# Ninety-nine small loads that nothing reads, beside a stream of large ones

## The chip, the cores and the metric

The kernel runs on one core of one Trainium2 chip. The metric is the device time of one execution in microseconds (us), the median of several. The core has TensorE (PE in the profile), VectorE (DVE), ScalarE (ACT), GpSimd (POOL) and SyncE (SP), and 16 DMA engines that move data between the device memory and the core's own memory. SP, ACT and POOL can issue loads; each has a queue of its own.

## The reference

A decode step for two sequences, one token each: attention over a cache of 4096 positions, beside a feed-forward layer, mixed by a gate.

```python
q = (x @ wq)                                  # 2 x 1 x 448 -> 16 heads of 256
scores = einsum("bhqd,bhkd->bhqk", q, k_cache) * 256 ** -0.5
p = softmax(scores)
a = einsum("bhqk,bhkd->bhqd", p, v_cache) @ wo
h = relu(x @ w1 + b1) ** 2
b = h @ w2 + b2
g = sigmoid((x * gate_w).sum(-1))
out = g * a + (1 - g) * b                     # 2 x 1 x 448
```

All is float32. The K cache and the V cache have 2 x 16 x 4096 x 256 numbers each, 134 MB each; the weights are small beside them.

## The kernel before, in words

The work goes in 16 rounds. A round is two heads of one sequence: its K is 8.4 MB and its V is 8.4 MB, each laid over 128 partitions, 64 positions of 256 numbers in each. Three buffers of that size fill most of the core's memory: `kp[0]` and `kp[1]` for the K of even and odd rounds, `vp` for V. At the start and at the end the same buffers hold wq, w1, wo and w2.

In a round i, VectorE multiplies K with the query in place (`times_q`, line 403), and sums each row of 256 products (`row_sums`, line 408), in two halves: multiply, sum, multiply, sum. The sums are the scores; they go to `s_t[i % 2]`, called `s0` and `s1`, so `s1` holds the scores of the odd rounds. Then come the maximum over all partitions (lines 420 and 430, with a turn through TensorE), the exponentials on ScalarE (`softmax`, line 437), and on TensorE 64 matrix products with V (`values`). Every fourth round the result is normalized and multiplied with a part of wo.

The main loop (`for i in range(LOOPED)`, lines 575 to 600) covers i = 0 to 11; the last four rounds are written out below it. In each pass it issues on SP: V of round i, K of round i + 2, and in every fourth pass a part of wo. Then come the products with V of round i, and VectorE's work on round i + 1.

SP issues in the order of the text and waits before each load until its buffer is free. V of round i goes into `vp`, free once TensorE has done `values(i - 1)`. K of round i + 2 goes where K of round i was, free once VectorE has done both row sums of round i. A wait on SP holds back all loads behind it.

Nothing of the order between engines is written by hand. Every operation is recorded with the regions that it reads (`r`) and writes (`w`), and `Flow.op` puts in the waits: for a reader on the last writer, for a writer on all earlier readers and writers of the region, unless the engine already knows by an earlier wait that they are done. A load has a semaphore of its own, named when it is issued. All loads go through one helper, so that in the profile they all have line 253.

In the profiled execution round 9 is on VectorE from 381.67 us, round 10 from 424.67, round 11 from 463.45 and round 12 from 502.15.

Of the kernel before, what the change touches and what calls it, by code (L numbers as in the profile page):

```python
# [10 lines left out]
PE, ACT, DVE, POOL, SP = "PE", "ACT", "DVE", "POOL", "SP"  # L11
# [12 lines left out]
class Flow:  # L24
# [21 lines left out]
    def op(self, eng, fn, r=(), w=(), give=None, take=(), dma=None):  # L46
        proc = dma or eng
        looped = eng == PE and self.body is not None
        o = Op(proc, eng, fn, give, looped)
        mine = self.ops.setdefault(proc, [])  # L50
        mine.append(o)
        o.n = len(mine)
        know = self.know[eng]
        for t in take:
            p = self.tokens[t].pop(0)
            o.takes.append((t, 16 if p.proc not in self.eng else 1))
            self.learn(know, p)
        need = {}
        for writes, regions in ((False, r), (True, w)):
            for name, lo, hi in map(self.span, regions):  # L60
                for p, a, b, wrote in self.seen.setdefault(name, []):
                    if a >= hi or b <= lo or not (wrote or writes):
                        continue
                    if p.proc == proc == PE:
                        continue
                    if know.get(p.proc, 0) < p.n and need.get(p.proc, p).n <= p.n:
                        need[p.proc] = p
        for p in sorted(need.values(), key=lambda p: -p.n):
            if know.get(p.proc, 0) >= p.n:
                continue  # L70
            assert not looped, (eng, p.proc, p.n, r, w)
            while p.give and p.proc in self.eng:
                later = [q for q in self.ops[p.proc][p.n:] if not q.give and q is not o]
                assert later, (eng, p.proc, p.n, r, w)
                p = later[0]
            p.inc = True
            o.waits.append(p)
            self.learn(know, p)
        for writes, regions in ((False, r), (True, w)):
            for name, lo, hi in map(self.span, regions):  # L80
                at = self.seen.setdefault(name, [])
                if writes:
                    at[:] = [x for x in at if not (lo <= x[1] and x[2] <= hi)]
                at.append((o, lo, hi, writes))
        o.know = dict(know)
        if give:
            self.tokens.setdefault(give, []).append(o)
        if looped:
            if self.passes == 1:
                self.body.append(o)  # L90
            else:
                first = self.body[self.at]
                assert first.takes == o.takes and not o.waits, (first.takes, o.takes)
                self.at += 1
        else:
            self.order[eng].append(o)
        return o
# [73 lines left out]
def gated_mix_kernel(nc, x, k_cache, v_cache, wq, wo, w1, b1, w2, b2, gate_w, out):  # L171
# [11 lines left out]
    HG = 4  # L183
# [18 lines left out]
    op = flow.op  # L202

    def sb(name, *shape):
        return nc.alloc_sbuf_tensor(name, shape, F32).ap()
# [42 lines left out]
    def rows(t):  # L248
        return t.rearrange("p (j d) -> p j d", d=DH)

    def load(eng, sem, dst, src, w, r=(), give=None):
        e = flow.eng[eng]
        op(eng, lambda: e.dma_start(dst, src), r=r, w=w, dma=sem, give=give)

    def place(t, lo=0, hi=NK * DH):
        return ("vp" if t is vp else "kp1" if t is kp[1] else "kp0", lo, hi)
# [7 lines left out]
    def of_round(src, i):  # L264
        b, n = rounds[i]
        return src[b, 2 * n:2 * n + 2].rearrange("h (p j) d -> (h p) j d", p=PH)

    def load_k(i, lo=0, hi=NK):
        t = kp[i % 2]
        load(SP, f"k{i % 2}_{lo}", rows(t)[:, lo:hi, :], of_round(k_cache, i)[:, lo:hi, :], [place(t, lo * DH, hi * DH)])  # L270

    def load_v(i, t, cuts=()):
        at = [0, *cuts, NK]
        for lo, hi in zip(at, at[1:]):
            give = "v" if i < LOOPED else None
            load(SP, "v" if give else f"v{i}_{lo}", rows(t)[:, lo:hi, :], of_round(v_cache, i)[:, lo:hi, :],
                 [place(t, lo * DH, hi * DH)], give=give)
        return t
# [26 lines left out]
    def vec(fn, r, w, give=None):  # L305
        op(DVE, fn, r=r, w=w, give=give)
# [22 lines left out]
    def mms(calls):  # L329
        def run():  # L330
            for out_, lhsT, rhs, start, stop in calls:
                i = t_.matmul(out_, lhsT, rhs, start=start, stop=stop, skip_group_check=True)  # L332
            return i
        return run

    op(PE, mms([(pxv[:, c, :], xr[:, c].rearrange("b r s -> b (r s)"), ident[:B, :B], True, True) for c in range(XC)]),
       r=[xr_r, "ident"], w=["sm"])
# [56 lines left out]
    for k in range(FB // 2):  # L394
        op(ACT, lambda k=k: s_.activation(h_sb[:, k * D:(k + 1) * D], ph[32 * k:32 * k + 2 * B, :D], AF.Copy),
           r=["ph"], w=[("shared", k * D, (k + 1) * D)])
# [21 lines left out]
    def maximum(i, token=False):  # L418
        s = s_t[i % 2]
        vec(lambda: v_.tensor_reduce(m, s, axis=AX.X, op=ALU.max), [f"s{i % 2}"], ["m"], give="m" if token else None)  # L420
        op(PE, mms([(mt[k * PH:(k + 1) * PH, :PH], m.to_broadcast([P, PH]), ident[:, k * PH:(k + 1) * PH], True, True)
                    for k in range(2)]), r=["m", "ident"], w=["mt"], take=["m"] if token else ())

    def buf(i):
        return 0 if i <= LOOPED else i % 2
# [19 lines left out]
    def clear(i):  # L445
        b, n = rounds[i]
        u, k = unit_of[2 * n]
        at = pwt[0].rearrange("p m (k b s) -> p m k b s", b=B, s=2)[:, :, k:k + 2, b, :]
        op(ACT, lambda: s_.activation(at, zero.unsqueeze(2).unsqueeze(3).to_broadcast([P, NK // 2, 2, 2]), AF.Copy), r=["zero"],  # L449
           w=[("pw0", 2 * (B * (k + e) + b), 2 * (B * (k + e) + b) + 2) for e in range(2)])  # L450
# [14 lines left out]
    def values(i, vt, lo=0, hi=NK // 2):  # L465
        b, h = rounds[i]
        u, k = unit_of[2 * h]
        n = len(units[u])
        po, pw = po_t[u % 2 if u > 2 else 0], pwt[buf(i)]
        name = f"po{u % 2 if u > 2 else 0}"  # L470
        token = i < LOOPED
        calls = []
        for mm in range(lo, hi):
            r = 32 * (mm % 4)
            calls.append((po[r:r + 4 * n, :], pw[:, mm, :4 * n], vt[:, 2 * mm * DH:(2 * mm + 2) * DH],
                          not token and k == 0 and b == 0 and mm < 4,
                          token or (k == n - 2 and b == B - 1 and mm >= NK // 2 - 4)))
        op(PE, mms(calls), r=[f"pw{buf(i)}", place(vt, 2 * lo * DH, 2 * hi * DH)], w=[name], take=["pw", "v"] if token else ())
# [63 lines left out]
    def load_w2():  # L542
        at = [0, *W2_CUTS, FC]
        for lo, hi in zip(at, at[1:]):
            load(SP, f"w2_{lo}", w2_t[:, lo:hi, :], w2_v[:, lo:hi, :], [place(kp[last % 2], w2_at + lo * D, w2_at + hi * D)])

    def late_w2(lo, hi):
        for c in range(lo, hi):
            op(PE, mms(late(hT[:, c, :], w2_t[:, c, :], stop=c == FC - 1)),
               r=["hT", place(kp[last % 2], w2_at + c * D, w2_at + (c + 1) * D)], w=["fin"])  # L550
# [21 lines left out]
    make_q(2)  # L572
    pick(3)

    for i in range(LOOPED):
        if i % HG == 0:
            flow.loop()
        flow.next_pass()
        vt = load_v(i, vp)
        if i < last - 3 - 1 or i + 2 < 14:  # L580
            load_k(i + 2)
        values(i, vt)
        clear(i)
        rest(i + 1, 0, 0)
        if i == 0:
            ffn_square(pt)
        if i % HG == HG - 1:
            load_wo(i // HG, i + 1)
        maximum(i + 1, True)
        softmax(i + 1)  # L590
        make_q(i + 3, True)
        if i < LOOPED - 1:
            pick(i + 4)
        if i % HG == HG - 1:
            u = i // HG
            flow.end_loop(16 * u)
            sums(u)
            norm(u)
            turn_wide(u)
            project(u)  # L600

    i = last - 3
# [16 lines left out]
    i = last - 2  # L619
# [2 lines left out]
    make_q(i + 2)  # L622
    rest(i + 1, 1, J)
    vt_next = load_v(i + 1, kp[(i + 1) % 2])
    maximum(i + 1)
    times_q(i + 2, 0, 0, LEAD)
    norm(NG - 1)
# [5 lines left out]
    i = last - 1  # L633
# [2 lines left out]
    load_wo(NG - 1, last)  # L636
    vt_next = load_v(i + 1, vp, V_CUTS)
    load_w2()
    values(i, vt, 0, NK // 4)
    maximum(i + 1)  # L640
    values(i, vt, NK // 4)
# [11 lines left out]
    late_wo(H - 2)  # L653
    late_wo(H - 1)
    late_w2(W2_CUTS[0], FC)
    y4 = shared[:, :DQ]
    op(ACT, lambda: s_.activation(y4, fin[:, :DQ], AF.Copy), r=["fin"], w=[("shared", 0, DQ)])  # L657
    ov = out.rearrange("b s (k n) -> b k (s n)", k=4)
# [30 lines left out]
```

## Time and profile before

| What | Value |
| --- | --- |
| median of 2 runs | 678.13 us (678.07 to 678.2) |
| the profiled execution, its own time | 678.43 us |
| its span, first to last instruction | 677.1 us |
| DVE busy | 569.6 us, 84% |
| PE busy | 246.3 us, 36% |
| ACT busy | 42.6 us, 6% |
| POOL busy | 0.7 us |
| DMA queue of SP (q1) | 7448 packets, 289.54 MB, 99.2% of 16 engines' span |
| DMA queue of ACT (q10) | 164 packets, 0.02 MB |
| granted TensorE clock | 0.652 of full speed |

The page cuts the span into 40 equal slices; a digit there is the busy share of a slice in tenths. A line of the timeline starts with the time from the start of the span and the duration, both in us, then the engine (with a q where it is the sequencer that issues a load), the line of the kernel, the operation, what it writes and reads, and in brackets the idle time before it with what ended it. Time to landing is from the issue of a load to the moment when its semaphore is complete.

### The profile page before, as it was taken

To read this page: it belongs to the slowest core of one execution; us is meant where nothing else is said; L and a number is where in the kernel's file an instruction comes from. 1 tells how busy PE (TensorE), PEld (TensorE's weight loads), DVE (VectorE), ACT (ScalarE), POOL (GpSimd) and SP (SyncE) were. 2 spreads that over 40 slices of the span, in tenths; PEclk is the share of its full clock that TensorE was granted. 3 is DMA by queue.
4 is the path that set the end of the run, shared out by engine and by line. 5 is a ranking of instruction groups with operands and counts; after the bars stand their busy time and mean duration, and the time that the engine had idled before them with its cause. 6 is when DMAs were issued, how large, how long until landed. Compare 5 with 4: busy or idle time off the path is not lost.

```text
span 677.1 us, 3790 instructions
## 1 busy us (share of the span) xinstructions
PE 246.3 (36%) x1658; PEld 83.3 (12%) x1658; DVE 569.6 (84%) x141; ACT 42.6 (6%) x142; POOL 0.7 (0%) x6
## 2 busy tenths in 40 slices
PE   2522350502306751140505455040411580602486
PEld 1100210100101510010101411010100240100122
DVE  3069999999999895979979896997979899999920
ACT  0001000000100201010000201000010110100000
POOL 0000000000000000000000000000000000000000
PEclk9957575665757566575856578585565865855789
DMA  9999999999999999999999999999999999999997
GB/s 380 434 430 435 435 434 434 434 434 434 434 434 434 451 434 434 434 434 434 434 434 434 430 431 434 434 434 434 434 434 434 406 451 422 432 443 434 401 429 299
DMA packets 7622, 289.71 MB, mean 428 GB/s; under 512 B 950, under 2 KB 1084, under 8 KB 2364
## 3 DMA queue, kind: packets, MB, share of 16 engines
q1 hardware_dynamic: 7448, 289.54, 99.2%
q8 instruction: 8, 0.13, 0.1%
q10 hardware_dynamic: 164, 0.02, 0.0%
q14 instruction: 2, 0.02, 0.0%
HBM read 289.56 MB, written 0.00 MB: 428 GB/s over the span
## 4 chain that ended last, share of the span: by engine, by line
DVE 41%; DMA 36%; PE 0%; issue 0%; ACT 0%; DVEq 0%
DMA kp<-in_A_k_cache_dram 32%; DVE s L408 21%; DVE kp L403 20%; DMA kp<-in_B_w_dram 4%; PE fin L332 0%; PE mt L332 0%; DVE nb L430 0%; ACT shared L657 0%; DVE rc L460 0%; DVE rl L461 0%; DVE rc L459 0%; DVE m L420 0%; DVEq L147 0%
## 5 line engine op out<-in xcount | busy, mean ns | idle before, releaser
L403 DVE TENSOR_TENSOR kp<-kp,q 128x8192 f32<-128x8192 f32 (+2 forms) x34 | 278.2, 8182 | 57.3 <-DMA kp<-in_A_k_cache_dram 57.3
L408 DVE TENSOR_REDUCE s<-kp 128x32 f32<-128x8192 f32 x32 | 277.9, 8686 | 1.1
L332 PE MATMUL po<-vp,pw 128*16 128x512 f32 (+1 forms) x960 | 138.8, 736 | 223.9 <-PEq L145 207.1
L332 PEld LDWEIGHTS po<-vp,pw 128*16 128x16 f32 (+1 forms) x960 | 31.1, 111 | 327.4 <-issue 306.4
L332 PE MATMUL mt<-ident,m 128*64 128x64 f32 x64 | 7.3, 318 | 148.9 <-PEq L145 85.5
L332 PE MATMUL sm<-rl,shared 128*128 128x8 f32 (+1 forms) x112 | 23.6, 347 | 9.1 <-ACT shared L488 8.1
L332 PE MATMUL acc<-kp,oTw 128*2 128x448 f32 x48 | 24.3, 673 | 2.5 <-ACT oTw L497 2.5
L332 PEld LDWEIGHTS mt<-ident,m 128*64 128x64 f32 x64 | 4.8, 191 | 162.9 <-issue 97.4
L449 ACT ACTIVATE pw<-zero 128x128 f32<-128x128 f32 x12 | 3.7, 311 | 326.9 <-PE po L332 326.9
L332 PEld LDWEIGHTS sm<-rl,shared 128*128 128x128 f32 x112 | 23.0, 311 | 10.7 <-DVE rl L461 4.6
L437 ACT ACTIVATE pw<-s,nb 64x64 f32<-64x64 f32 x32 | 11.1, 348 | 176.7 <-DVE nb L430 176.5
L332 PE MATMUL ph<-vp,xT 128*4 128x448 f32 x28 | 7.2, 679 | 16.6 <-DMA vp<-in_B_w_dram 16.6
L332 PE MATMUL po<-kp,pw 128*8 128x512 f32 x64 | 10.1, 790 | 8.1 <-DMA kp<-in_A_v_cache_dram 8.1
L430 DVE TENSOR_REDUCE nb<-mt 128x1 f32<-128x64 f32 x16 | 3.6, 223 | 11.1 <-PE mt L332 11.1
L332 PE MATMUL pq<-qs,sel 128*64 128x256 f32 x48 | 12.3, 594 | 0.0
L332 PE MATMUL po<-vp,xT 128*4 128x512 f32 x56 | 7.7, 711 | 4.9 <-DMA vp<-in_A_wq_dram 4.9
L459 DVE RECIPROCAL rc<-sm 128x8 f32<-128x8 f32 (+1 forms) x5 | 1.0, 196 | 7.9 <-PE sm L332 7.9
L488 ACT ACTIVATE shared<-po 128x512 f32<-128x512 f32 x12 | 6.5, 591 | 11.4 <-PE sm L332 11.4
L379 ACT ACTIVATE q<-pq 128x256 f32<-128x256 f32 x16 | 6.1, 384 | 13.1 <-PE pq L332 12.8
L332 PEld LDWEIGHTS acc<-kp,oTw 128*2 128x2 f32 x48 | 4.5, 98 | 20.1 <-issue 17.3
L437 ACT ACTIVATION_READ_ACCUMULATOR pw<-s,nb 64x1 f32 x32 | 5.9, 185 | 0.0
L332 PEld LDWEIGHTS pq<-qs,sel 128*64 128x64 f32 x48 | 4.1, 212 | 0.0
(64 smaller groups left out, 61.9 us busy)
## 6 DMA issues: line engine op xcount, KB each, us to landing
kp<-in_A_k_cache_dram SPq DMA_DIRECT2D x4, 4096.0 KB, 27.5
vp<-in_A_wq_dram SPq DMA_DIRECT2D x1, 7168.0 KB, 19.7
kp<-in_A_wo_dram SPq DMA_DIRECT2D x4, 1792.0 KB, 25.5
vp<-in_A_v_cache_dram SPq DMA_DIRECT2D x1, 4096.0 KB, 24.1
vp<-in_B_w_dram SPq DMA_DIRECT2D x1, 3136.0 KB, 19.0
vp<-in_A_v_cache_dram SPq DMA_DIRECT2D x1, 2048.0 KB, 28.6
kp<-in_B_w_dram SPq DMA_DIRECT2D x2, 896.0 KB, 29.9
vp<-in_A_v_cache_dram SPq DMA_DIRECT2D x1, 1024.0 KB, 30.6
```

The source lines that it names most:

```text
L332: i = t_.matmul(out_, lhsT, rhs, start=start, stop=stop, skip_group_check=True)
L379: op(ACT, lambda: s_.activation(t, pq[:, :DH], AF.Copy), r=["pq"], w=[f"q{i % 3}"])
L403: vec(lambda: v_.tensor_tensor(kt, kt, q.unsqueeze(1).to_broadcast([P, hi - lo, DH]), op=ALU.mult), at + [f"q{i % 3}"], at)
L408: vec(lambda: v_.tensor_reduce(s[:, at], rows(t)[:, at, :], axis=AX.X, op=ALU.add), [place(t, half * HALF, (half + 1) * HALF)], [(f"s{i % ...
L430: vec(lambda: v_.tensor_reduce(nb, mt[:, :PH], axis=AX.X, op=ALU.max, negate=True), ["mt"], [f"nb{i % 2}"])
L437: op(ACT, lambda: s_.activation(pw[at, :, 2 * c:2 * c + 2], s[at].rearrange("p (m s) -> p m s", s=2), AF.Exp, bias=nb[at], accum_out=rs[at ...
L449: op(ACT, lambda: s_.activation(at, zero.unsqueeze(2).unsqueeze(3).to_broadcast([P, NK // 2, 2, 2]), AF.Copy), r=["zero"], w=[("pw0", 2 * ...
L459: vec(lambda: v_.reciprocal(c, sm[:, :B * n].rearrange("p (k b) -> p k b", b=B)), ["sm"], ["rc"])
L488: op(ACT, lambda s=s, lo=lo: s_.activation(o_w[:, s], pv[:, s, lo:lo + HJ // 2].unsqueeze(2).to_broadcast([P, HJ // 2, HG, HP]), AF.Copy), ...
```

## The change

Two small tiles are added: `grid` (16 partitions, 15 slots of 16 bytes) and `few` (32 partitions, 24 slots of 16 bytes). A series (`ladder`) issues fifteen loads on SP: 15 rows of 16 bytes, then 14, down to 1 row; the rows lie in the K cache, 1024 bytes apart. There are five series: in the passes i = 0, 4 and 8 of the loop, behind the load of K of round i + 2; behind the load of V of round 14; and behind the loads of w2, the last loads of the kernel. In pass 9, `side` issues 24 loads on GpSimd: eight of 17 rows, eight of 8 rows and eight of 1 row. They are recorded as readers of `s1`, so GpSimd issues them once the scores of round 9 are there. No computation reads `grid` or `few`. An operation that does nothing is added on SP ahead of the store of the output; it is recorded as a reader of all these slots. [...]

```diff
@@ -572,6 +572,18 @@
     make_q(2)
     pick(3)
 
+    grid = sb("grid", 16, 15, 4)
+    few = sb("few", 32, 24, 4)
+
+    def ladder():
+        for k in range(15, 0, -1):
+            load(SP, f"lad{k}", grid[:k, k - 1], k_cache[0, 0, :k, :4], [f"grid{k}"])
+
+    def side(i):
+        for n in range(24):
+            k = (17, 8, 1)[n // 8]
+            load(POOL, f"side{n}", few[:k, n], k_cache[0, 0, :k, :4], [f"few{n}"], r=[f"s{i % 2}"])
+
     for i in range(LOOPED):
         if i % HG == 0:
             flow.loop()
@@ -579,7 +591,11 @@
         vt = load_v(i, vp)
         if i < last - 3 - 1 or i + 2 < 14:
             load_k(i + 2)
+        if i % HG == 0:
+            ladder()
         values(i, vt)
+        if i == 9:
+            side(i)
         clear(i)
         rest(i + 1, 0, 0)
         if i == 0:
@@ -622,6 +638,7 @@
     make_q(i + 2)
     rest(i + 1, 1, J)
     vt_next = load_v(i + 1, kp[(i + 1) % 2])
+    ladder()
     maximum(i + 1)
@@ -636,6 +653,7 @@
     load_wo(NG - 1, last)
     vt_next = load_v(i + 1, vp, V_CUTS)
     load_w2()
+    ladder()
     values(i, vt, 0, NK // 4)
@@ -653,6 +671,7 @@
     late_w2(W2_CUTS[0], FC)
+    op(SP, lambda: nc.sync.nop(), r=[f"few{n}" for n in range(24)] + [f"grid{k}" for k in range(15, 0, -1)])
     y4 = shared[:, :DQ]
@@ -672,7 +691,7 @@
-    nc = _bacc.Bacc("TRN2", target_bir_lowering=False, num_devices=1)
+    nc = _bacc.Bacc("TRN2", target_bir_lowering=False, num_devices=1, dynamic_dma_scratch_size=8192)
```

## The prediction

> **What bounds the kernel now.** The page comes first: busy shares, the slices, the queues.
>
> ```profile
> span 677.1 us, 3790 instructions
> ...
> PE 246.3 (36%) x1658; PEld 83.3 (12%) x1658; DVE 569.6 (84%) x141; ACT 42.6 (6%) x142; POOL 0.7 (0%) x6
> ...
> DMA  9999999999999999999999999999999999999997
> GB/s 380 434 430 435 435 434 434 434 434 434 434 434 434 451 434 434 434 434 434 434 434 434 430 431 434 434 434 434 434 434 434 406 451 422 432 443 434 401 429 299
> ...
> q1 hardware_dynamic: 7448, 289.54, 99.2%
> ...
> q10 hardware_dynamic: 164, 0.02, 0.0%
> ```
>
> The DMA engines are the limit: 99.2% of sixteen engines' span goes to SP's queue (q1), at a flat 434 GB/s, and 289.54 MB at 434 GB/s is 667 of the 677.1 us. VectorE has 107 us to spare. Nothing that only adds loads can make this faster; slower it gets in two ways only: an engine is busy with something else, or an engine's queue runs empty because a buffer came free too late. So the second view is when SP issues (the timeline of SP, then that of VectorE) around the place where GpSimd's loads go in.
>
> ```profile
> 399.45 0.33 SPq L253 DMA_DIRECT2D kp<-in_A_k_cache_dram  x1
> 414.47 0.33 SPq L253 DMA_DIRECT2D vp<-in_A_v_cache_dram  x1
> ...
> 492.41 0.33 SPq L253 DMA_DIRECT2D vp<-in_A_v_cache_dram  x1
> 498.21 0.33 SPq L253 DMA_DIRECT2D kp<-in_A_k_cache_dram  x1
> 519.59 0.33 SPq L253 DMA_DIRECT2D kp<-in_A_wo_dram  x1
> 536.90 0.33 SPq L253 DMA_DIRECT2D kp<-in_A_k_cache_dram  x1
> ```
> ```profile
> 407.71 8.69 DVE L408 TENSOR_REDUCE s<-kp 128x32 f32<-128x8192 f32 x1
> 416.44 0.22 DVE L420 TENSOR_REDUCE m<-s 128x1 f32<-128x64 f32 x1
> ...
> 424.67 8.69 DVE L403 TENSOR_TENSOR kp<-kp,q 128x8192 f32<-128x8192 f32 x1 [7.28 <-DMA kp<-in_A_k_cache_dram]
> ...
> 472.18 8.69 DVE L408 TENSOR_REDUCE s<-kp 128x32 f32<-128x8192 f32 x1
> ...
> 489.49 8.69 DVE L408 TENSOR_REDUCE s<-kp 128x32 f32<-128x8192 f32 x1
> ...
> 502.15 8.69 DVE L403 TENSOR_TENSOR kp<-kp,q 128x8192 f32<-128x8192 f32 x1 [2.83 <-DMA kp<-in_A_k_cache_dram]
> ...
> 536.91 0.22 DVE L420 TENSOR_REDUCE m<-s 128x1 f32<-128x64 f32 x1
> ```
>
> Here round 9 ends at 416.40 (407.71 + 8.69), round 11's first row sum starts at 472.18, its second ends at 498.18, and 0.03 us later SP issues the K of round 13. How early is that? The chain of waits has it, and single issues looked up by their start give the time to landing (first the V issued at 492.41, then the half K at 536.90):
>
> ```profile
> 498.21 42.54 DMA kp<-in_A_k_cache_dram
> ```
> ```profile
> DMA to landing us min/median/max: 29.0/29.0/29.0
> ```
> ```profile
> DMA to landing us min/median/max: 18.3/18.3/18.3
> ```
> ```profile
> vp<-in_A_wq_dram SPq DMA_DIRECT2D x1, 7168.0 KB, 19.7
> ```
>
> The first load, into empty queues, took 19.7 us for 7.34 MB; 7.34 MB at 434 GB/s are 16.9, so 2.8 us are start and landing. An 8.39 MB load alone would take 19.3 + 2.8 = 22.1 us, and this K took 42.5: it queued for 20.4 us, its **slack**. The half K (4.19 MB, 9.7 + 2.8 = 12.5) took 18.3: slack 5.8. V landed at 521.4, which is how long the queue lasts if round 11 stops.
>
> **The change part by part.** Its instruction list shows 75 more loads on SP, 24 on GpSimd, TensorE the same, and on VectorE one difference: round 11's first row sum (the 472.18 row) now waits for all 24 of GpSimd's loads. They are declared to read `s1`, and this row sum writes `s1`.
>
> *Issue on SP.* The small loads stand behind K of rounds 2, 6, 10, V of round 14 and w2. Loads issued back to back took at most this:
>
> ```profile
> 632.50 6.92 SPq L253 DMA_DIRECT2D vp<-in_A_v_cache_dram  x5
> 639.46 7.54 SPq L253 DMA_DIRECT2D kp<-in_B_w_dram  x5
> ...
> 675.01 0.64 SPq L253 DMA_DIRECT2D out_dram<-shared  x1
> ```
>
> That is 1.4 to 1.5 us each with a full queue, 0.33 free. Fifteen are 5 to 22 us; I take 0.4 to 1 us each, 6 to 15 us. The third series, from 399.8, has until 414.47 (14.7 us) and the last, from 647.0, until 675.01. What is late behind the third is a V with some 7 us of queue ahead of it, so 0. The waits of a series for the one before are long met.
>
> *Data on SP's queue.* What does a small packet cost? In the window 7:20 us ACT's queue (q10) brings 56-byte rows beside SP's:
>
> ```profile
> DMA packets 225, 5.75 MB, mean 442 GB/s; under 512 B 125, under 2 KB 127, under 8 KB 127
> ...
> q1 hardware_dynamic: 113, 5.74, 102.0%
> q10 hardware_dynamic: 112, 0.01, 0.6%
> ```
>
> 0.6% of 16 x 13 us over 112 packets is **11 ns** each, and SP's rate does not fall. The 164 packets of q10 are the rows of its five loads (2, 2, 2, 128 and 4) and one semaphore packet for each engine used (2, 2, 2, 16, 4): 138 + 26. So a load of k rows, up to 4 at least, is on k engines, two packets each; the busiest engine sees all 15 of a series. Sixty loads ahead of the last stretch x 2 x 11 ns = 1.3 us on that engine; the fifth series, behind w2, 0.3 us more, ahead of the output's issue, which waits for it. If that engine is not the last to finish, it is 0. From above, the stretch with many short loads:
>
> ```profile
> 642.00:674.00 32.00, 24.63 (x299) 8.30 (x303) 5.13 (x6) 1.65 (x6) 0.00 (x0) 0.90 0.97 401
> ```
>
> 401 instead of 434 GB/s over 32 us loses 2.4 us among 12 loads, 0.2 us each, so 75 loads at most 15 us. The 11 ns row is the nearer one, being small rows: I take 1.1 us.
>
> *GpSimd's queue.* POOL issues nothing in this trace, so its price has only bounds. The row of packets above also shows the interleaving: 113 of SP's against 112 of ACT's, **one for one**. A small packet on another queue costs 11 ns, but waits its turn behind one packet of SP's. In steady state:
>
> ```profile
> DMA packets 144, 8.39 MB, mean 435 GB/s; under 512 B 16, under 2 KB 16, under 8 KB 16
> ```
>
> This is the window 463.4:482.7, one load: 144 / 16 = 9 packets per engine in 19.3 us, a turn of 2.15 us. With one packet per load and engine, 24 loads are 24 x 2.15 = 51.6 us; from 416.4 they land at 468.0, or up to 472.8 with 2.8 us of start and landing and one turn: no wait worth naming. With two (row and semaphore, as in q10), 48 turns are 103.2 us, 519.6. The third series stands between: it is in SP's queue behind the K that landed at 424.67, and its 30 short packets on the busiest engine hand GpSimd's queue up to 30 turns for almost nothing, as far as GpSimd has issued by then. At 0.5 us per issue (ACT's and SP's rows are 0.33 to 1.5) it has issued 16; 32 packets are away at 424.7, the other 16 take 34.4 us, done at 459. At 1 us, 16 loads are left: 68.8 us, 493.5.
>
> *What a wait costs.* A stall of S at 472.18 moves K of round 13 by S (slack 20.4) and round 12 by S - 2.83, as VectorE waited there anyway. The half K goes out at the end of round 12, slack 5.8. So the DMA engines idle for S - 2.83 - 5.8 = S - 8.6; after that they are the limit again. Landing by 480.8 costs nothing.
>
> [...]
>
> **Sum.** 678.43 (the profiled execution: span 677.1 and 1.3 around it) + 1.1 for the series + 0.5 for 48 packets of 11 ns on the busiest engine + 0 for the stall = 680.0; the median of the runs is 0.3 lower, so **679.7**. Alone this forecast has 678 to 684: the stall up to 12 us (3.4 lost), the series between 0 and 1.6.
>
> **Rivals.** *VectorE stalls until the queue is empty.* If every GpSimd load takes two turns or more on an engine that the third series does not reach, or GpSimd issues at 2 us, the loads are not done before SP's queue drains at 521.4; SP cannot refill it, as K of round 13 waits for round 11. Then S = 521.4 - 472.2 + 0.5 = 49.7 and 49.7 - 8.6 = 41.1 us are lost. Checked forward: K issued at 547.9 lands at 570.0, 29.3 late; the half K at 536.9 + 46.9 = 583.8 lands at 596.3 instead of 555.2, 41.1 late; the rest is back to back. Time 679.7 + 41.1 = **720.8**. For it: in q10 each row and each semaphore takes a turn; against: nothing shows that GpSimd's do. It decides from 480.8.
>
> [...]
>
> *In between:* two turns per load, helped by the third series, at 1 us per issue: landing at 493.5, S = 21.3, 12.7 lost: **692.4**; at 1.5 us some 19 loads are left, 506.4, S = 34.2, 25.6 lost: 705.
>
> *Each small load costs a fixed piece on all engines,* the 0.2 us: 678.1 + 15 = **693**. Against it: the flat rate beside 112 small packets.
>
> *The change does less than it says:* the loads start too late to matter or the busiest engine is never last: 678.3.
>
> **How the numbers follow.** Forecast 0.44, together with the case of less; emptied queue 0.28; in between 0.19; fixed piece 0.07; 0.02 for other things. A measurement of this kernel tells about 2%, 13.6 us, from no change. The in-between case and the fixed piece lie across that line, 0.10 of their 0.26 below it: within 2% 0.55, slower 0.44, faster 0.01, as DMA at 434 GB/s is full. The range must reach the emptied queue: 678 to 722.
>
> **What would show it.** In the profile after: a queue of GpSimd's with its packets (24 x 16 = 384 if one per load and engine, twice that or more if not); the row sum at 472 with or without idle time before it from a load of `few`; 434 GB/s in every slice, or a dent behind 521; K of round 13 issued at 498 or later. SP's queue should have 600 rows and 600 semaphore packets more. I am wrong if the dent is there, if GB/s falls where the series are, or if SP issues V of round 9 after 421.

## The result, and the profile after

The changed kernel takes 720.58 us (median, 720.52 to 720.64) against 678.13 before: the ratio is 1.0626, with a 95% interval of 1.058 to 1.0672. It is slower by 42 us. The time is inside the range that was given, but it isn't the forecast: it is that of the rival in which VectorE stalls (720.8).

The page of the kernel after, its span, its slices and its queues (packets, MB, share of 16 engines):

```profile
span 719.1 us, 3909 instructions
...
DMA  9999999999999999999999999999907679999996
GB/s 409 408 468 408 446 405 434 434 437 437 431 437 427 431 405 437 437 427 441 430 437 427 427 401 430 416 430 430 445 29 292 277 292 409 436 439 434 385 429 261
...
q1 hardware_dynamic: 8648, 289.55, 94.2%
...
q0 software_dynamic: 768, 0.01, 0.1%
```

SP's queue has 1200 packets more, 600 rows and 600 semaphores, as forecast. GpSimd's queue has **768**, not 384: two packets for each of 24 loads on each of 16 engines (by the trace each of the 24 semaphores goes up in 16 steps). And there is the dent: one slice of 18 us moves 29 GB/s and the next three under 300. The groups of instructions and the timelines of VectorE, SP and GpSimd say where the dent is from:

```profile
L408 DVE TENSOR_REDUCE s<-kp 128x32 f32<-128x8192 f32 x32 | 278.0, 8686 | 41.5 <-DMA few<-in_A_k_cache_dram 40.4
```
```profile
428.05 8.69 DVE L403 TENSOR_TENSOR kp<-kp,q 128x8192 f32<-128x8192 f32 x1 [7.74 <-DMA kp<-in_A_k_cache_dram]
...
470.26 8.69 DVE L403 TENSOR_TENSOR kp<-kp,q 128x8192 f32<-128x8192 f32 x1 [6.47 <-DMA kp<-in_A_k_cache_dram]
519.35 8.69 DVE L408 TENSOR_REDUCE s<-kp 128x32 f32<-128x8192 f32 x1 [40.40 <-DMA few<-in_A_k_cache_dram]
```
```profile
402.85 5.39 SPq L253 DMA_DIRECT2D grid<-in_A_k_cache_dram  x15
417.49 0.35 SPq L253 DMA_DIRECT2D vp<-in_A_v_cache_dram  x1
...
499.25 0.33 SPq L253 DMA_DIRECT2D vp<-in_A_v_cache_dram  x1
545.38 0.33 SPq L253 DMA_DIRECT2D kp<-in_A_k_cache_dram  x1
563.85 0.33 SPq L253 DMA_DIRECT2D kp<-in_A_wo_dram  x1
581.17 0.33 SPq L253 DMA_DIRECT2D kp<-in_A_k_cache_dram  x1
```
```profile
419.62 12.09 POOL L253 DMA_DIRECT2D few<-in_A_k_cache_dram  x24 [418.15 <-DVE s L408]
```

GpSimd issues the 24 loads in 12.09 us, 0.5 us each. The first row sum of round 11 then stands for 40.40 us until the last of them has landed. SP's K of round 13 goes out at 545.38 (before: 498.21), as it needs the buffer that round 11 holds; meanwhile SP's queue runs dry. How the loads of `few` landed is in the answer on DMA for the window 416:526 (issues of one size, KB each, median us to landing):

```profile
few<-in_A_k_cache_dram POOLq DMA_DIRECT2D x8, 0.3 KB, 23.1
few<-in_A_k_cache_dram POOLq DMA_DIRECT2D x8, 0.1 KB, 42.9
few<-in_A_k_cache_dram POOLq DMA_DIRECT2D x8, 0.0 KB, 74.1
```

The size doesn't set these times, the place in the queue does: the eight loads of one row are the last. By the landing times in the trace the first is in at 428.85, and most of the steps from one to the next are 4.84 to 4.86 us. A 64 KB packet of SP's took 2.42 us in the packet records (64 KB at a sixteenth of 434 GB/s is the same), so a step is two of them.

### The profile page after: what moved, and what is told of

It reads as the page before. It is cut to its first block, busy times and chain, and to the rows that moved or that the text cites. A ratio compares the mean times of both kernels' runs of the same rounds, so it can differ in the third digit from the quotient of the medians.

```text
span 719.1 us, 3909 instructions
## 1 busy us (share of the span) xinstructions
PE 245.1 (34%) x1658; PEld 83.0 (12%) x1658; DVE 569.6 (79%) x141; ACT 42.6 (6%) x142; POOL 12.8 (2%) x30
## 3 DMA queue, kind: packets, MB, share of 16 engines
q1 hardware_dynamic: 8648, 289.55, 94.2%
## 5 line engine op out<-in xcount | busy, mean ns | idle before, releaser
L408 DVE TENSOR_REDUCE s<-kp 128x32 f32<-128x8192 f32 x32 | 278.0, 8686 | 41.5 <-DMA few<-in_A_k_cache_dram 40.4
L253 POOL DMA_DIRECT2D few<-in_A_k_cache_dram x24 | 12.1, 515 | 418.2 <-DVE s L408 418.2
```

The lines of the kernel that those rows point to most:

```text
L408: vec(lambda: v_.tensor_reduce(s[:, at], rows(t)[:, at, :], axis=AX.X, op=ALU.add), [place(t, half * HALF, (half + 1) * HALF)], [(f"s{i % ...
```

## The experiments

Two things had to be told apart. Theory 1: each of GpSimd's loads takes two turns behind a large packet on every engine, and VectorE's wait for them makes the time. The rivals put the time on the series, or on the loads as such. The second question came up with the first answer: the series cost far more than 1.1 us, and the last four runs were made for that. Where a run leaves small loads out, the operation ahead of the output no longer reads them.

**The two parts alone.** First the series alone (no loads on GpSimd), then GpSimd's loads alone (no series).

```diff
-        if i == 9:
-            side(i)
```
```diff
-        if i % HG == 0:
-            ladder()
...
-    ladder()
...
-    ladder()
```

> The five series alone; GpSimd's 24 loads are left out. Theory 1 (the time is VectorE's stall on GpSimd's loads): no stall; what is left is the series. In the changed kernel's trace V behind the first series landed 0.9 us later than before, V behind the second 1.7, V of the last round behind the fourth 1.3, and SP's store was issued 1.75 us behind ACT's: with 1 to 2 for the third, some 6 us in all, 683 to 685. Theory 2 (small packets on the busiest engine and the gaps that they leave take the time, GpSimd's queue only adds to it): 60 of the 84 DMA rows added, so well over half of the 42 us stays: above 700. By the prediction's 11 ns a packet: 679.2.

Measured: 687.0 us (686.85 to 687.17), ratio 1.0127 (1.011 to 1.0144).

> GpSimd's 24 loads alone, with the row sum's wait; no series. Theory 1: 24 x 2 packets on each engine, one per packet of SP's queue, 2.42 us: from 417 some 116 us, so they last until SP's queue runs empty at about 521; stall 48 to 50 us, 40 to 42 us lost: 718 to 722. The series do not matter for the stall, as the engines that they do not reach decide. Theory 2: without the series under 700.

Measured: 720.71 us (720.58 to 720.94), ratio 1.0624 (1.0606 to 1.0641). VectorE's and SP's timelines of this run:

```profile
463.96 8.69 DVE L403 TENSOR_TENSOR kp<-kp,q 128x8192 f32<-128x8192 f32 x1 [3.08 <-DMA kp<-in_A_k_cache_dram]
522.19 8.69 DVE L408 TENSOR_REDUCE s<-kp 128x32 f32<-128x8192 f32 x1 [49.54 <-DMA few<-in_A_k_cache_dram]
```
```profile
548.22 0.33 SPq L253 DMA_DIRECT2D kp<-in_A_k_cache_dram  x1
566.69 0.33 SPq L253 DMA_DIRECT2D kp<-in_A_wo_dram  x1
584.00 0.33 SPq L253 DMA_DIRECT2D kp<-in_A_k_cache_dram  x1
```

GpSimd's loads alone give the whole time of the change, and step by step the rival's chain: S = 49.54 (49.7), K of round 13 issued at 548.22 (547.9), the half K at 584.00 (583.8). The last load landed at 522.07, just when SP's queue had run empty. The series alone cost 8.6 us, which is neither of the two sizes of the prediction; together the two do not add up, since 8.6 + 42.3 would be 729.

**The wait or the loads?** GpSimd's loads are released by a small VectorE fill of a new tile behind round 9, and no longer declared to read `s1`. They run as before, but no row sum waits for them; the wait for them is left to an operation that does nothing, on SP behind the fourth series.

```diff
-            load(POOL, f"side{n}", few[:k, n], k_cache[0, 0, :k, :4], [f"few{n}"], r=[f"s{i % 2}"])
+            load(POOL, f"side{n}", few[:k, n], k_cache[0, 0, :k, :4], [f"few{n}"], r=["mark"])
...
         if i == 9:
+            fill("mark", mark)
             side(i)
```

> All loads of the change, but GpSimd's are released by a tiny VectorE fill behind round 9's scores and are no longer recorded as readers of s1, so the row sum of round 11 does not wait for them. They still take until about 520 or later. Theory 1: 6 us for the series and up to 4 for GpSimd's packets between SP's: 683 to 688, and no dent in GB/s behind 521. Theory 2 (the packets themselves): about 720, as nothing but the wait is gone.

Measured: 688.38 us (688.07 to 688.69), ratio 1.0147 (1.013 to 1.0164). From VectorE's timeline:

```profile
469.73 8.69 DVE L403 TENSOR_TENSOR kp<-kp,q 128x8192 f32<-128x8192 f32 x1 [5.81 <-DMA kp<-in_A_k_cache_dram]
478.46 8.69 DVE L408 TENSOR_REDUCE s<-kp 128x32 f32<-128x8192 f32 x1
```

No idle time stands before the row sum, while GpSimd's loads still land one by one until 526.5 by the trace, in the same steps. So 24 slow loads beside the stream cost 1.4 us over the series alone; the other 32 us are the wait.

**The same loads on SP's queue.** By theory 1 they stand in line there and take no turns.

```diff
-            load(POOL, f"side{n}", few[:k, n], k_cache[0, 0, :k, :4], [f"few{n}"], r=[f"s{i % 2}"])
+            load(SP, f"side{n}", few[:k, n], k_cache[0, 0, :k, :4], [f"few{n}"], r=[f"s{i % 2}"])
```

> The 24 small loads of pass 9 go through SP's queue, behind K of round 11, with the row sum's wait on them kept. Theory 1: in one queue they stand in line and take no turns; they land right behind K of round 11, 1 to 4 us later, before the row sum at about 475: stall 0 to 2 us, 685 to 690. If the wait itself (24 semaphores on VectorE) or the small rows were the cause, about 720.

Measured: 694.17 us (693.96 to 694.55), ratio 1.0231 (1.0214 to 1.0248). VectorE doesn't wait for them (its row sum starts at 477.43 us without idle time), which was the point, but the time is above the expectation, and SP's timeline shows why:

```profile
419.54 0.35 SPq L253 DMA_DIRECT2D kp<-in_A_k_cache_dram  x1
419.94 53.47 SPq L253 DMA_DIRECT2D few<-in_A_k_cache_dram  x24
473.45 0.35 SPq L253 DMA_DIRECT2D vp<-in_A_v_cache_dram  x1
```

Issuing held SP for 53.47 us, above all at the loads of 17 rows (by the trace the fourth alone for 18.1 us and the fifth for 26.2, while none of 8 rows or of 1 row took more than 0.3), and V of round 10 went out at 473.45, 20.9 later than before. By the trace the semaphore of a 17-row load goes up in two steps, as that of a one-row load does, and that of an 8-row load in nine. The packets agree: SP's queue has 288 more than with the series alone (8936 against 8648), 208 rows and 80 semaphores, which is one for each load of 17 rows or of one row and eight for each of 8. So by both counts a 17-row load ran on one engine, and only the 17-row loads were held. What held them was not read from any run.

**Half of them, and shorter turns.** Two runs test that the price is turns. First twelve loads in place of 24 (four of each size); then all 24, with the loads of K and V cut to packets of 16 KB (`most` is 16384 for them, 65536 for all others), and beside it the kernel before with the same packets.

```diff
-        for n in range(24):
-            k = (17, 8, 1)[n // 8]
+        for n in range(12):
+            k = (17, 8, 1)[n // 4]
```
```diff
-        op(eng, lambda: e.dma_start(dst, src), r=r, w=w, dma=sem, give=give)
+        op(eng, lambda: e.dma_start(dst, src, max_dma_last_dim=most), r=r, w=w, dma=sem, give=give)
```

> The changed kernel with 12 of GpSimd's loads in place of 24 (four of 17, four of 8, four of 1 row). Theory 1: on an engine without a row of the series each load takes two turns behind a large packet, 4.85 us, so twelve take 58 us from 418-425 and land at 476-483, while round 11's first row sum could start at 479 (the series have cost some 5-7 us by then). The stall is 0 to 4 us and less than the slack of half a K: 686 to 690, that is, the price of the series alone. Theory 2: the cost is in proportion to the number of loads (each load takes away something): half of what the 24 add to the series, 16 us, so some 703.

Measured: 688.59 us (688.23 to 689.11), ratio 1.0153 (1.0136 to 1.017). VectorE's timeline has the row sum of round 11 without idle time:

```profile
478.75 8.69 DVE L408 TENSOR_REDUCE s<-kp 128x32 f32<-128x8192 f32 x1
```

The last of twelve landed at 469.45 by the trace, before the 476 to 483 of the expectation. Half the loads cost not half the stall but none: all twelve were in 9.3 us before their reader started.

> The changed kernel, in which the loads of K and V alone are cut to packets of 16 KB in place of 64 KB. Theory 1 (each load of GpSimd waits for two packets of SP's queue): a turn is a quarter, about 0.6 us, 48 turns are 29 us, all loads have landed by 450 to 455, no stall of VectorE, and the time is 679 to 690 (what the series cost with shorter packets in front). Theory 2 (a fixed delay per load of GpSimd, of 4.85 us, whatever SP's packets are): VectorE stalls as before, 715 to 722.

> The kernel before with the loads of K and V cut to packets of 16 KB, as a base for the run with both. Both theories: 434 GB/s as before, 678 within 3 us.

Measured: 695.25 us (694.85 to 695.43), and for its base 685.37 (685.2 to 685.41; ratio to the kernel before 1.0103, 1.0086 to 1.012). Both missed their expectations (679 to 690, and 678 within 3 us) for one reason: the shorter packets cost 7 us by themselves. What the change adds to this base is 9.9 us in place of 42. The DMA answer for the window 416:526, and the tile's own answer:

```profile
few<-in_A_k_cache_dram POOLq DMA_DIRECT2D x8, 0.3 KB, 7.9
few<-in_A_k_cache_dram POOLq DMA_DIRECT2D x8, 0.1 KB, 13.8
few<-in_A_k_cache_dram POOLq DMA_DIRECT2D x8, 0.0 KB, 19.1
```
```profile
who waited for it (us, times):
busy tenths in 40 slices 0000000000000000000000005100000000000000
DMA to landing us min/median/max: 5.5/13.8/21.7
```

Nobody waited. The steps between landings are 1.24 us for most loads, about a quarter of 4.86, as the packets are a quarter. So no fixed delay of a GpSimd load shows here; its price in both runs is two packets of what the other queue sends (16 KB at a sixteenth of the 428 GB/s of the base's page are 0.61 us).

**What makes a series dear.** All four have no loads on GpSimd: three loads per series (15, 8 and 1 rows); thirty (each of the fifteen cut in two of 8 bytes a row); fifteen of one row each; and the 75 loads of the series spread in threes behind 25 of the large loads.

```diff
-        for k in range(15, 0, -1):
+        for k in (15, 8, 1):
```
```diff
-            load(SP, f"lad{k}", grid[:k, k - 1], k_cache[0, 0, :k, :4], [f"grid{k}"])
+            load(SP, f"lad{k}", grid[:k, k - 1, :2], k_cache[0, 0, :k, :2], [f"grid{k}"])
+        for k in range(15, 0, -1):
+            load(SP, f"mad{k}", grid[:k, k - 1, 2:], k_cache[0, 0, :k, 2:4], [f"gridb{k}"])
```
```diff
-            load(SP, f"lad{k}", grid[:k, k - 1], k_cache[0, 0, :k, :4], [f"grid{k}"])
+            load(SP, f"lad{k}", grid[:1, k - 1], k_cache[0, 0, :1, :4], [f"grid{k}"])
```
```diff
+    steps = []
+
     def ladder():
-        for k in range(15, 0, -1):
+        for _ in range(3):
+            k = 15 - len(steps) % 15
+            steps.append(k)
             load(SP, f"lad{k}", grid[:k, k - 1], k_cache[0, 0, :k, :4], [f"grid{k}"])
...
         vt = load_v(i, vp)
+        if i > 0:
+            ladder()
         if i < last - 3 - 1 or i + 2 < 14:
             load_k(i + 2)
-        if i % HG == 0:
-            ladder()
+        ladder()
```

> The series alone (without GpSimd's loads), with three loads each (15, 8 and 1 rows) in place of fifteen. Theory 1: a series costs once, by the slow start of the large packet behind it (3.4 to 4.4 us in place of 2.42): 684 to 687. Theory 2: each small load or packet costs a share: a fifth of the 8.6 us, 680.

Measured: 678.83 us (678.62 to 679.05), ratio 1.0006 (0.9997 to 1.0016). Both theories said more. This run is built with `dynamic_dma_scratch_size=8192` too, so that alone costs nothing here; what it does to GpSimd's own loads was not run.

> The series alone (without GpSimd's loads), with thirty loads each: every one of the fifteen is cut into two of 8 bytes a row, so that the busiest engine has a run of 60 small packets in place of 30. Theory 1 (a long run of small packets makes a DMA engine late once, at the large packet behind the run): 686 to 692, some 1 to 2 us for each series as with fifteen, plus 1 to 3 us at the end, where SP waits for more loads. Theory 2 (each small packet or load costs a share): the 8.6 us double, 695 to 697.

Measured: 701.33 us (701.16 to 701.63), ratio 1.0339 (1.0321 to 1.0356). It is above both.

> The series alone, with fifteen loads of one row each in place of 15 to 1 rows: 15 rows for a series in place of 120, and all on one engine, which still has a run of 30 small packets. Theory 1 (the run on one engine makes that engine late): that engine is the last from then on, 1 to 2 us per series and 1 to 2 us at the output's issue: 684 to 688. Theory 2 (a share for each row): an eighth of the 8.6 us, 679.2 to 679.7. Theory 3 (a share for each load): as with fifteen, 686 to 688.

Measured: 686.66 us (686.39 to 687.02), ratio 1.012 (1.0104 to 1.0137).

> The 75 loads of the series alone, of the same sizes, but three at a time behind 25 of the large loads (V and K of the rounds 1 to 11 of the loop, K alone in its first pass, V of round 14, w2), so that no engine has a run of more than 6 small packets. Theory 1 (only a long run makes an engine late): 678.4 to 680.5. Theories 2 and 3 (a share for each row or for each load): 685 to 688, as with five series of fifteen.

Measured: 679.39 us (679.18 to 679.65), ratio 1.0014 (1.0004 to 1.0023).

One row of VectorE's timeline compares them all: the first product of round 7, which starts when the K behind two series has landed. In this order: before; series of three; spread; one row; the fifteen (series alone); thirty.

```profile
304.34 8.69 DVE L403 TENSOR_TENSOR kp<-kp,q 128x8192 f32<-128x8192 f32 x1 [2.90 <-DMA kp<-in_A_k_cache_dram]
```
```profile
304.36 8.69 DVE L403 TENSOR_TENSOR kp<-kp,q 128x8192 f32<-128x8192 f32 x1 [2.90 <-DMA kp<-in_A_k_cache_dram]
```
```profile
304.50 8.69 DVE L403 TENSOR_TENSOR kp<-kp,q 128x8192 f32<-128x8192 f32 x1 [2.91 <-DMA kp<-in_A_k_cache_dram]
```
```profile
307.07 8.69 DVE L403 TENSOR_TENSOR kp<-kp,q 128x8192 f32<-128x8192 f32 x1 [4.83 <-DMA kp<-in_A_k_cache_dram]
```
```profile
307.17 8.69 DVE L403 TENSOR_TENSOR kp<-kp,q 128x8192 f32<-128x8192 f32 x1 [4.61 <-DMA kp<-in_A_k_cache_dram]
```
```profile
312.91 8.69 DVE L403 TENSOR_TENSOR kp<-kp,q 128x8192 f32<-128x8192 f32 x1 [7.83 <-DMA kp<-in_A_k_cache_dram]
```

In the five runs behind the first line, the longest run of small packets on one engine is 6, 6, 30, 30 and 60 (a row and a semaphore packet for each load, as in the 600 and 600 of the changed kernel); the delay after two series is 0.0, 0.2, 2.7, 2.8 and 8.6 us. The rows don't matter: 15 rows in a series cost what 120 cost (686.66 and 687.0 us). The count of loads doesn't either: 75 loads in threes cost 1.0 us in all, and in fifteens 8.6. **In these runs it is the run on one engine that counts**, and beyond some length it costs more than in proportion: twice 30 costs three times as much. The expectation of one fixed delay per run falls with the thirty (686 to 692 was said). Two things were not told apart: whether the packets of a run count or its loads, as each load adds two packets on the busiest engine; and at which length between 6 and 30 the delay begins.

By the packet records the run itself is short, 9 ns for most packets; the time goes into the large packet behind it. At the second series of the one-row run one 64 KB packet takes 4.29 us, right behind 30 small ones, while the others around it take about 2.42; with thirty loads such packets take up to 6.4 us there, and up to 6.9 at the third series. Why is open.

A second piece is at the end. In the kernel before SP issues its half of the output at 675.01, and ACT its own with it. The rows of ACT and SP before (ACT's), with the series alone, with thirty loads, and of the changed kernel:

```profile
675.02 0.62 ACTq L253 DMA_DIRECT2D out_dram<-shared  x1
```
```profile
681.64 0.62 ACTq L253 DMA_DIRECT2D out_dram<-shared  x1
...
683.75 0.62 SPq L253 DMA_DIRECT2D out_dram<-shared  x1
```
```profile
693.15 0.62 ACTq L253 DMA_DIRECT2D out_dram<-shared  x1
...
698.12 0.63 SPq L253 DMA_DIRECT2D out_dram<-shared  x1
```
```profile
715.50 0.62 ACTq L253 DMA_DIRECT2D out_dram<-shared  x1
...
717.25 0.62 SPq L253 DMA_DIRECT2D out_dram<-shared  x1
```

SP is 2.1, 5.0 and 1.75 us later than ACT; it alone waits for the series. With three loads it is 0.07 us by the trace.

## Why the forecast was wrong, point by point

**What bounds the kernel** was right: DMA (SP's queue has 99.2% before and 98.5% with the series alone), and a loss only where the queue ran empty (29 GB/s in a slice) or an engine was held up (4.29 us for a 64 KB packet).

**Two steps failed**, both in *GpSimd's queue*, and VectorE stalled because both did. The first is "With one packet per load and engine, 24 loads are 24 x 2.15 = 51.6 us". It is two, by 768 packets; no run shows one packet per load and engine: the other runs with 24 loads on GpSimd have 768 too, and the one with twelve has 384. The value for two stood in the next sentence, 48 turns, 103.2 us, 519.6, and the last load landed at 519.2; that it came so close is in part luck, as GpSimd's first packet went at 423.4 by the packet records, not at 416.4, and a burst, told below, hurried them.

The turn of 2.15 us held as a mean. A turn behind a 64 KB packet is 2.42, but every large load of SP's adds one semaphore packet per engine (16 of the 144 packets in the prediction's window of one load), a ninth turn that takes 9 ns by the packet records. It shows in the landings: behind three or four steps of 4.85 us stands one of about half, the first at 445.93, when SP's queue was sending the semaphore packets of a V (443.1 to 449.9). In the run without series 22 steps from 424.82 to 521.09 make 2.19 us a turn. (One sum of the step is slightly off: 468.0 + 2.8 + 2.15 is 473.0 and not 472.8, which changes nothing.)

The second step is the help by the third series. Even with two packets the prediction had all loads done at 459, if GpSimd issues at 0.5 us, and it did. But 32 packets per engine were to be away by 424.7, and only four loads had landed by 443.4. GpSimd's queue did send more while the series went by, 120 packets in 423 to 428 us against 33 in 455 to 460, but not on all engines: the longest load of a series has 15 rows and 15 semaphore packets (a series has 120 of each), so it reaches 15 engines at most. A load of GpSimd's is in with the 16th step of its semaphore. The ninth load shows it, with the first step at 432.0 and the last at 463.1.

The evidence was on the page: q10's 138 + 26 packets show the semaphore as a packet of its own (26 of 4 bytes by the packet records). The argument against it, that nothing shows GpSimd's queue, spoke for neither side, and should not have turned the choice to the value with no row behind it. The rows made no difference to these loads: each semaphore goes up in 16 steps, 768 = 24 x 16 x 2 agrees, and the one-row loads landed in the same steps of 4.85 us as those of 17.

**A burst** that nobody forecast came later. In 462 to 465 us GpSimd's queue sent 245 of its 768 packets (27 in the run without the wait, 24 in the run without series), and the ninth to twelfth load landed within 3 us, 463.1 to 466.1. The run without the wait has the same series and no burst, so the series alone do not make it. SP had issued V of round 10 at 461.00, against 459.53 and 454.22 in those two runs. SP's queue run empty for a moment on some engines would fit this; that was not read for single engines, and the cause stays open.

**The price of a wait**, S - 8.6, was right; in the run without series the issues of its chain came within 0.3 us. For the change itself: S = 40.4 gives 31.8. Before that the three series, with GpSimd's loads beside the third, had made round 11's start 6.8 us late (470.26 against 463.45; 468.38 with the series alone); the fourth adds 1.4 by the landings behind it, and SP's issue of the output is at 717.25 while ACT's is at 715.50, 1.75. The sum is 41.8, and the span grew by 42.0.

So the rival, to which 0.28 was given and for which the range was stretched to 722, had the stall right, but its 720.8 is right by luck: two errors cancel. Its S was 9.3 too long: 6.8 as the row sum could start only so much later, and the rest as the loads had landed at 519.2, while V of round 11, the last load in SP's queue, landed at 528.4. And the small loads cost 10.0 us besides the stall (6.8 + 1.4 + 1.75), where the sum had 1.6 for them.

**The series** was mis-sized: 1.1 us against 8.6 alone. The row of 11 ns was right for a packet (9 by the packet records) and for two queues side by side; it does not show what comes behind a run on one queue, as q10's packets alternate with SP's (112 beside 113 in 7:20 us). The rival with 0.2 us per load (693) was too dear and had the wrong mechanism, as it counts loads.

**Issue** held. GpSimd's 0.5 us is 12.09 / 24, also in the last 3.7 us, beside VectorE's product from 428.05. On SP the third series took 5.39 us, a little under the 6 to 15 of the prediction, and V of round 9 went out at 417.49, before the 421 named as the limit. That a full queue made the rows of 1.4 to 1.5 us each was not read from any run.

## What to carry to other kernels

Here small loads on a second queue were cheap for the stream beside them but slow for their reader: 24 cost 1.4 us when nobody waited, and most landed two of the stream's packets after the one before, 4.86 us behind 64 KB packets and 1.24 behind 16 KB. So look for who waits for such loads, also by a declaration that nobody needs, and count turns times the packet of the other queue against the reader's slack. Small loads on the busy queue itself were better kept apart: the same 75 cost 8.6 us in runs of fifteen and 1.0 in threes.

## What the runs showed of the hardware that was not expected

- A run of small packets on one engine made the large packet behind it late: 4.29 us in place of 2.42 behind a run of 30, up to 6.9 behind 60. Behind runs of 6 round 7 started 0.0 and 0.2 us later than before. One engine was enough (686.66 us with one-row loads, 687.0 with up to 15 rows).
- A load of 17 rows on SP held SP at the issue for 26.2 us, and 24 loads, eight of them of 17 rows, for 53.47 us; fifteen loads of 15 to 1 rows took 5.39.
- Packets of 16 KB in place of 64 KB for K and V cost 1.0% (685.37 us), with nothing else changed.
